# Batch 0 of a fused block-sparse attention and SwiGLU kernel: three groups of 256 queries in place of two of 384, with part of its data movement put on DMAs

## The chip, the cores and the metric

The kernel runs on one core of a Trainium2 chip. The metric is device microseconds (us) of one execution; the time before is the median of three runs. A core has five engines with a queue each: PE (TensorE, matrix products; its weight loads are listed as PEld), DVE (VectorE), ACT (ScalarE), POOL (GpSimd) and SP (SyncE). An instruction waits at the head of its queue until what it depends on is done, and all that stand behind it in that queue wait too. SP does nothing here but start DMAs, POOL does little else.

## What is computed

Attention over 4 batches of 8 heads, 768 positions and 64 features; then, over the 8 x 64 = 512 features of each position, an RMS norm and a gated feed-forward network (FFN):

```python
scores = scale * np.matmul(q, k.transpose(0, 1, 3, 2))        # q, k, v: (4, 8, 768, 64)
# mask, in blocks of 32: |blk_i - blk_j| <= 1, first and last block row and column, 3 sampled blocks a row
scores = np.where(mask, scores, -1000000000.0)
attn = softmax(scores);  x = np.matmul(attn, v)                # then (3072 tokens, 512)
xn = x / np.sqrt(np.mean(x * x, axis=-1, keepdims=True) + 1e-06) * rms_g
g = xn @ w_gate                                               # (512, 1536)
out = (g * sigmoid(g) * (xn @ w_val)) @ w_out                 # (1536, 512), float32
```

## The kernel before

**Groups.** `groups` is a list of eight (batch, half): each batch's 768 queries in two groups of `TG` = 384, that is three tiles of 128. The main loop (L501 on) goes through the groups, and in each through the 8 heads h.

**One head of one group.** `scores` (L276) makes the scores of two of the six key tiles: two matmuls from `KT` and `QT` into a PSUM tile `st` (two buffers), and one exponential on ACT into `ex`. It is called three times a head. `KT` and `QT` hold 64 rows of features and, under them, 24 rows (D:KR) that add the mask: block indicators for the keys (`kind`), 0 or -65536 for the queries (`qmask`). They exist twice, for batches of even and odd number. `pv` (L286) then makes 18 matmuls for the head *before* (its `ex` must be there), and DVE divides by the row sums into `stage`. After a group's last `pv`, `squares` sums the squares on DVE, `rms_power` (L307) raises them on POOL to `rstd`, `rms_scale` (L316) scales on DVE to `xs`, and `xs` is turned to `xg` with the features on the partitions: on PE (`transpose_x`, L328) for the first two groups and the last, else by DMA transposes that SP issues (L321), after a factor `gain` has been multiplied in.

**The FFN as filling.** A group's FFN (`ffn_pieces`, L344) is 36 pieces: for each of 12 slices of the hidden width a `gate` and a `val` of four matmuls each, then 12 pieces `down` of three matmuls. They go into a list `fill` when `xg` is ready, that is at head `TX` = 2 of the following group, and `position()`, called four times a head between `scores` and `pv`, takes 36/32 of a piece each time. So while PE works on group n's attention, it also works on group n-1's FFN. While there is no FFN (all of group 0, and group 1 up to head 2: `thin`), `keep_busy` (L142) puts matmuls of zeros in the gaps. `down`'s last part ends with a copy on ACT (`yo`) and the DMA to the output on SP (L387).

**Loads.** All loads of q, k, v and of the three weights go through POOL's queue, with a cast to bfloat16 except for v, in program order: batch 0's pairs of heads, `wg` and `wv` in two halves each, then at head 4 of group 0 two pairs of batch 1, then `wo` (L451). The first two heads come through SP (`first`). The mask rows of batch 0 are computed once and copied to the other heads by DVE (`copy_rows`, L216); those of the second `KT` and `QT` by two DMAs on SP (L454).

**Turning q and k.** q and k arrive with positions on partitions and are turned in pairs of heads. Batches 0 and 1: on PE (`transpose_qk`, L243: six transposes, then two copies on DVE), batch 1 at the places in `TURNS_0` (L488). Batches 2 and 3: `turn` (L261) starts a DMA transpose on SP into a buffer `turned`, and one head later `place` (L269) starts two DMAs on SP that copy from there to `KT` or `QT`. `place` must wait, at the head of SP's queue, until the transpose has landed. Four such turns stand in each group of 384:

```python
if turned:
    place(*next(iter(turned)))
if 0 < b < B - 1 and h >= 4:
    turn(b + 1, 2 * g + (h - 4) // 2, h % 2)
```

The order on every queue is that of the program: the schedule is written by hand (`tc.manual_schedule()`).

Of the kernel before, what the change touches and what calls it, by code (L numbers as in the profile page):

```python
# [17 lines left out]
def kernel(  # L18
# [30 lines left out]
    TG = HC * P  # L49
# [75 lines left out]
    def first_turn(t16, unread=None):  # L125
        t = ps_f.tile([P, HC, P], BF16, name="tfirst", tag="ff")
        for cc in range(HC):
            nc.tensor.transpose(
                out=t[:, cc, :], in_=t16[:, 2 * cc * D:(2 * cc + 2) * D], identity=ident)
        if unread is not None:  # L130
            keep_busy(2, 256, unread)
        return t

    def first_copy(h, which, t, w, copy):
        dst = (KT if which == 0 else QT)[0]
        view = dst[0:D, h, :].rearrange("p (c w s) -> p c w s", w=2, s=P)
        copy(out=view[:, :, w, :], in_=t[w * D:(w + 1) * D])
# [71 lines left out]
    def mask_queries(half):  # L209

        lo, hi = half * HC, (half + 1) * HC
        nc.vector.tensor_copy(
            out=qmask.rearrange("p (c r) -> p c r", c=NC)[:, lo:hi, :],
            in_=qnat[0:NB, :].rearrange("p (r c) -> p c r", c=NC)[:, lo:hi, :])
# [8 lines left out]
    mask_keys(0, 2)  # L223
# [8 lines left out]
    kt = first_turn(k16, unread)  # L232
    q16 = first_cast(0, 1)
    qt = first_turn(q16, unread)
    keep_busy(5, 256, unread)
    for which, t in ((0, kt), (1, qt)):
        first_copy(0, which, t, 0, nc.scalar.copy)
        first_copy(0, which, t, 1, nc.vector.tensor_copy if which else nc.scalar.copy)
    second16 = [first_cast(1, which) for which in range(2)]
    mask_keys(2, NC)  # L240


    def transpose_qk(b, pr, which, spare=False):  # L243


        src = (kbf if which == 0 else qbf).pop((b, pr))
# [3 lines left out]
        for e in range(2):  # L250
            for cc in range(HC):
                nc.tensor.transpose(  # L252
                    out=t[:, e, cc, :], in_=src[:, e, 2 * cc * D:(2 * cc + 2) * D],
                    identity=ident)
        view = dst[0:D, 2 * pr:2 * pr + 2, :].rearrange("p e (c w s) -> p e c w s", w=2, s=P)
        for w in range(2):
            nc.vector.tensor_copy(out=view[:, :, :, w, :], in_=t[w * D:(w + 1) * D])  # L257
# [18 lines left out]
    def scores(b, g, h, j2, ex):  # L276
        st = ps_s.tile([P, 2, 512], FP32, name="st", tag="st")
        for e in range(2):
            jt = 2 * j2 + e
            nc.tensor.matmul(  # L280
                out=st[:, e, 0:TG], lhsT=KT[b % 2][0:KR, h, jt * P:(jt + 1) * P],
                rhs=QT[b % 2][0:KR, h, g * TG:(g + 1) * TG], start=True, stop=True)
        nc.scalar.activation(  # L283
            out=ex[:, 2 * j2:2 * j2 + 2, :], in_=st[:, :, 0:TG], func=AF.Exp, scale=SCALE)

    def pv(b, h, ex, stage):  # L286
        op = ps_o.tile([P, HC, 80], FP32, name="op", tag="ot")
        for it in range(HC):
# [5 lines left out]
        nc.vector.reciprocal(out=rz, in_=op[:, :, D])  # L294
        nc.vector.tensor_tensor(  # L295
            out=stage[:, :, h * D:(h + 1) * D], in0=op[:, :, 0:D],
            in1=rz.unsqueeze(2).to_broadcast([P, HC, D]), op=ALU.mult)
# [9 lines left out]
    def rms_power(e):  # L307
        e["rstd"] = work.tile([P, HC], FP32, name="rstd", tag="rstd", bufs=2)
        nc.gpsimd.tensor_tensor(out=e["rstd"], in0=e["ssq"], in1=mhalf, op=ALU.pow)  # L309
        e["xs"] = work.tile([P, HC, DM], BF16, name="xs", tag="xs", bufs=2)  # L310
        e["xg"] = work.tile([P, KD, TG], BF16, name="xg", tag="xg", bufs=2)

    def by_dma(e):
        return e["bg"] not in (groups[0], groups[1], groups[-1])

    def rms_scale(e, it):  # L316
        if by_dma(e):
# [10 lines left out]
    def transpose_x(e, half):  # L328
        if by_dma(e):
            return  # L330
        xs, xg = e["xs"], e["xg"]
        t = ps_o.tile([P, 2, HC, P], BF16, name="tx", tag="ot")
        for w in range(2):
            c = 2 * half + w
            for it in range(HC):
                nc.tensor.transpose(  # L336
                    out=t[:, w, it, :], in_=xs[:, it, c * P:(c + 1) * P], identity=ident)
        for w in range(2):
            c = 2 * half + w
            nc.vector.tensor_scalar(  # L340
                out=xg[:, c, :], in0=t[:, w].rearrange("p c s -> p (c s)"),
                scalar1=rmsg[:, c:c + 1], scalar2=None, op0=ALU.mult)

    def ffn_pieces(gate_pool, b, g, xg, last=False):  # L344

        hps = work.tile([P, NF, TG], BF16, name="hps", tag="hps", bufs=2)
        held = {}

        def gate(f):
            gp = gate_pool.tile([P, 512], FP32, name="gp", tag="ff")  # L350
            for c in range(KD):
                nc.tensor.matmul(  # L352
                    out=gp[:, 0:TG], lhsT=wg[:, c, f * P:(f + 1) * P], rhs=xg[:, c, :],
                    start=(c == 0), stop=(c == KD - 1))
            th = work.tile([P, TG], BF16, name="th", tag="th", bufs=3)
            nc.scalar.activation(out=th, in_=gp[:, 0:TG], func=AF.Tanh, scale=0.5)  # L356
            held[f] = (gp, th)

        def val(f):
            gp, th = held.pop(f)  # L360
            vp = ps_f.tile([P, 512], FP32, name="vp", tag="ff")
            for c in range(KD):
                nc.tensor.matmul(  # L363
                    out=vp[:, 0:TG], lhsT=wv[:, c, f * P:(f + 1) * P], rhs=xg[:, c, :],
                    start=(c == 0), stop=(c == KD - 1))
            u = work.tile([P, TG], BF16, name="u", tag="u", bufs=3)
            nc.vector.scalar_tensor_tensor(  # L367
                out=u, in0=th, scalar=1.0, in1=gp[:, 0:TG], op0=ALU.add, op1=ALU.mult)
            nc.vector.tensor_tensor(out=hps[:, f, :], in0=u, in1=vp[:, 0:TG], op=ALU.mult)  # L369
# [5 lines left out]
        def down(tt, part, lo=0, hi=DM):  # L375
# [7 lines left out]
            if part == NQ - 1:  # L383
# [3 lines left out]
                nc.sync.dma_start(out=rows[g * HC + tt][:, lo:hi], in_=yo)  # L387
# [5 lines left out]
        for tt in range(HC):  # L393
            for part in range(NQ):
                if last and tt == HC - 1:
                    continue
                pieces.append(lambda tt=tt, part=part: down(tt, part))
        if last:
            for lo in range(0, DM, DM // 2):
                for part in range(NQ):  # L400
                    pieces.append(
                        lambda lo=lo, part=part: down(HC - 1, part, lo, lo + DM // 2))
# [3 lines left out]
    groups = [(b, g) for b in range(B) for g in range(2)]  # L406
    fill = []
    NPOS = 4 * H
    PER = 2 * NF + 4 * HC
    due = [0.0]  # L410

    def position():
        due[0] += PER / NPOS
# [8 lines left out]
    def after_pv(e, h):  # L422
        if h == H - 2:
            squares(e, 0, 0, (H - 1) * D)
        if h == H - 1:
            for it in range(HC):
                squares(e, it, (H - 1) * D, H * D)
            rms_power(e)


    def side_work(b, g, h):
        nb = b + 1
        if b == 0 and g == 0:
            if h % 2 == 0:
                cast_v(0, h // 2, nc.vector)
            if h == 0:
                copy_rows(KT, kind, 2, 4, 0, S)
                copy_rows(QT, qmask, 2, 4, 0, TG)
            if h == 1:
                load_gv(1)  # L440
            if h == 2:
                copy_rows(KT, kind, 4, H, 0, S)
            if h == 3:
                copy_rows(QT, qmask, 4, H, 0, TG)
                mask_queries(1)
            if h == 5:
                copy_rows(QT, qmask, 1, H, TG, S)
            if h == 4:
                load_qk(1, 0)
                load_qk(1, 1)  # L450
                nc.gpsimd.dma_start(out=wo, in_=moe_w_out.rearrange("(c p) f -> p c f", p=P))  # L451
            if h == H - 2:
                for T in (KT, QT):
                    nc.sync.dma_start(  # L454
                        out=T[1][D:KR, :, :],
                        in_=T[0][D:KR, H - 1, :].unsqueeze(1).to_broadcast([NB, H, S]))
            return
        if b == 0:
            if h == 1:
                load_v(1, 0)  # L460
                load_v(1, 1)
                for pr in range(2, NP):
                    load_qk(1, pr)
                nc.gpsimd.dma_start(
                    out=gain, in_=moe_rms_g.unsqueeze(0).to_broadcast([P, DM]))
            return

    def casts(b, g, h):


        if (b, g) == (0, 1):
            if h >= 6:
                cast_v(1, h - 6, nc.vector)
                load_v(1, h - 4)
            return
        if b == 0 or h not in (2, 4):
            return
        n = h // 2 - 1
        if g == 0:
# [3 lines left out]
        if b + 1 < B:  # L483
            load_v(b + 1, 2 * g + n)
            load_qk(b + 1, 2 * g + n)


    TURNS_0 = {(0, 1, 3): (0, 0), (0, 1, 4): (0, 1), (0, 1, 5): (1, 0), (0, 1, 6): (1, 1),  # L488
               (0, 1, 7): (2, 0), (1, 0, 0): (2, 1), (1, 0, 3): (3, 0), (1, 0, 4): (3, 1)}

    def turns(b, g, h):
        if (b, g, h) in TURNS_0:
            transpose_qk(1, *TURNS_0[(b, g, h)])
        if turned:
            place(*next(iter(turned)))
        if 0 < b < B - 1 and h >= 4:
# [4 lines left out]
    for gi, (b, g) in enumerate(groups):  # L501
# [3 lines left out]
            "bg": (b, g),  # L505
        }
        for h in range(H):
            ex = work.tile([P, NC, TG], BF16, name="ex", tag="ex", bufs=3)
            thin = gi == 0 or (gi == 1 and h <= TX)
            scores(b, g, h, 0, ex)  # L510
            if h == 0 and prev is not None:
                squares(prev[0], 2, 0, (H - 1) * D)
            if gi == 0 and h == 0:
                scores(b, g, h, 1, ex)
                second = [first_turn(t16) for t16 in second16]
                for which in range(2):
                    for w in range(2):
                        first_copy(1, which, second[which], w, nc.vector.tensor_copy)
                copy_rows(KT, kind, 1, 2, 0, S)
                copy_rows(QT, qmask, 1, 2, 0, TG)  # L520
                nc.vector.tensor_scalar(out=rmsg, in0=rmsg, scalar1=float(DM) ** 0.5,
                                        scalar2=None, op0=ALU.mult)
            if h == 1 and ending is not None:
                rms_scale(ending, 1)
            if h == TX and ending is not None:
                transpose_x(ending, 0)
            if gi == 0 and 0 < h < H - 2:
                transpose_qk(0, h // 2 + 1, h % 2, spare=True)
# [3 lines left out]
            if gi or h:  # L532
                scores(b, g, h, 1, ex)
            side_work(b, g, h)
            position()
            if h == 1 and ending is not None:
# [3 lines left out]
            if prev is not None:  # L540
                pe, pb, ph, pex = prev
                pv(pb, ph, pex, pe["stage"])
                after_pv(pe, ph)
                if ph == H - 1:
                    ending = pe
            position()
            scores(b, g, h, 2, ex)
            if gi == 0 and h == 0:
                transpose_qk(0, 1, 0, spare=True)
            position()  # L550
            if h == TX and ending is not None:
                transpose_x(ending, 1)
                fill.extend(ffn_pieces(ps_f, *ending["bg"], ending["xg"]))
                ending = None
            casts(b, g, h)
            turns(b, g, h)
            if gi == 2 and h == 0:
                nc.vector.tensor_scalar(out=gain, in0=gain, scalar1=float(DM) ** 0.5,
                                        scalar2=None, op0=ALU.mult)
            if h == 0 and ending is not None:  # L560
                rms_scale(ending, 0)
            if h == H - 1:
                squares(cur, 1, 0, (H - 1) * D)
            prev = (cur, b, h, ex)
    pe, pb, ph, pex = prev
    squares(pe, 2, 0, (H - 1) * D)
    pv(pb, ph, pex, pe["stage"])
# [15 lines left out]
    with tc.tile_pool(name="ps_tail", bufs=4, space=bass.MemoryType.PSUM) as ps_tail:  # L583
        for piece in ffn_pieces(ps_tail, *groups[-1], pe["xg"], last=True):
# [31 lines left out]
```

## Time and profile before

| what | value |
|---|---|
| median of three runs | 321.73 us (321.05 to 322.42) |
| the profiled execution's own time | 322.85 us |
| its span in the profile | 321.0 us |
| granted TensorE clock, mean | 0.995 |
| busy: PE, PEld, DVE, ACT, POOL | 309.9, 190.1, 208.9, 205.5, 47.1 us |
| first `gate` matmul of group 0 | 40.71 us after the span's start |
| first output DMA issued | 72.47 us |

The profile lists, per engine, what ran when, for how long, and what released each wait; times are from the span's start. "PEclk" is the clock that TensorE was granted, as a share of full speed. A PE instruction's listed duration is from its issue to the end of its results; in a stream the next one starts earlier, so that what one costs is read from the starts: four matmuls with 384 columns start 0.65 us apart from the next four. SPq rows are DMA starts in SP's queue, and their time is that of the issue, not that of the transfer. "q0" is the DMA queue fed by POOL, "q1" that fed by SP.

### The profile page before, as it was taken

Reading aid. Unit: us, or ns where it says so; the run is one execution under the profiler, and the core shown is the slowest. Engines: PE = TensorE matmul, PEld = TensorE weight load, DVE = VectorE, ACT = ScalarE, POOL = GpSimd, SP = SyncE. Lnnn points to the kernel's source line nnn. Section 1 sums busy time; section 2 is a strip of 40 time slices with the busy share of each in tenths; the row PEclk is TensorE's granted clock in tenths of the full one; section 3 lists DMA queues with packets and bytes.
Section 4 is the critical chain, followed back from the end, with each engine's and each line's share of the span. In section 5 each row is a group of like instructions: output and inputs, shape, how many; then the busy total and the mean of one; then the engine's idle time right before and its main releaser. Section 6 shows DMA issues by size and latency. Waiting matters only on the chain.

```text
span 321.0 us, 6990 instructions
## 1 busy us (share of the span) xinstructions
PE 309.9 (97%) x2779; PEld 190.1 (59%) x2779; DVE 208.9 (65%) x532; ACT 205.5 (64%) x321; POOL 47.1 (15%) x69
## 2 busy tenths in 40 slices
PE   8798799999999999999999999999999999999996
PEld 4465466655666556665566556665666556655554
DVE  6896667993787726684477727684477726693860
ACT  6678776655766667666766667666866667633322
POOL 9730600010220121100220121101000100010000
PEclk9889999999999999999999999999999999999999
DMA  7999994111696567837775456845200040002002
GB/s 153 297 219 224 210 257 82 45 55 67 131 140 84 65 173 131 166 63 108 163 124 100 92 149 117 151 88 107 66 2 0 19 133 0 2 1 100 1 0 100
DMA packets 52637, 33.57 MB, mean 105 GB/s; under 512 B 35620, under 2 KB 48316, under 8 KB 52604
## 3 DMA queue, kind: packets, MB, share of 16 engines
q0 software_dynamic: 13696, 17.17, 27.7%
q1 hardware_dynamic: 38872, 15.94, 22.5%
q8 instruction: 22, 0.36, 0.5%
q14 instruction: 11, 0.09, 0.1%
q10 hardware_dynamic: 36, 0.01, 0.0%
HBM read 28.59 MB, written 6.29 MB: 109 GB/s over the span
## 4 chain that ended last, share of the span: by engine, by line
PE 79%; DVE 12%; DMA 4%; POOL 1%; issue 1%; ACT 1%; SPq 0%; DVEq 0%; POOLq 0%
PE gp L352 18%; PE vp L363 17%; PE st L280 16%; PE yp L380 15%; PE op L290 10%; DVE junk L302 3%; DMA xg<-xs 2%; DMA vraw<-in_v_dram 2%; DVE hps L369 2%; DVE u L367 2%; DVE stage L295 1%; PE tqk L252 1%; PE unread L147 1%; PE tx L336 1%; DVE QT L257 1%
## 5 line engine op out<-in xcount | busy, mean ns | idle before, releaser
L283 ACT ACTIVATE ex<-st 128x768 bf16<-128x768 f32 x192 | 154.0, 811 | 57.2 <-PE st L280 54.5
L280 PE MATMUL st<-QT,KT 88*128 88x384 bf16 x384 | 93.8, 329 | 3.8 <-DVE QT L257 1.7
L352 PE MATMUL gp<-xg,wg 128*128 128x384 bf16 x384 | 78.4, 325 | 0.4 <-DMA xg<-xs 0.4
L363 PE MATMUL vp<-xg,wv 128*128 128x384 bf16 x384 | 78.1, 325 | 0.0
L367 DVE SCALAR_TENSOR_TENSOR u<-th,gp 128x384 bf16<-128x384 bf16 x96 | 53.0, 552 | 36.8 <-ACT th L356 35.5
L380 PE MATMUL yp<-wo,hps 128*128 128x512 bf16 (+1 forms) x300 | 73.8, 370 | 0.5 <-DVE hps L369 0.5
L356 ACT ACTIVATE th<-gp 128x384 bf16<-128x384 f32 x96 | 46.9, 489 | 35.4 <-PE gp L352 35.3
L369 DVE TENSOR_TENSOR hps<-u,vp 128x384 bf16<-128x384 bf16 x96 | 53.2, 554 | 10.4 <-PE gp L352 0.5
L280 PEld LDWEIGHTS <-KT 88*128 88x128 bf16 x384 | 36.6, 99 | 33.9 <-issue 4.4
L290 PEld LDWEIGHTS <-ex 128*128 128x128 bf16 x1152 | 45.4, 98 | 12.0 <-DVE KT L257 0.5
L363 PEld LDWEIGHTS <-wv 128*128 128x128 bf16 x384 | 36.2, 97 | 23.4
L352 PEld LDWEIGHTS <-wg 128*128 128x128 bf16 x384 | 35.7, 97 | 23.7 <-issue 0.9
L290 PE MATMUL op<-Vp,ex 128*128 128x65 bf16 x1152 | 47.7, 195 | 0.1
L380 PEld LDWEIGHTS <-hps 128*128 128x128 bf16 x300 | 27.7, 97 | 24.0 <-DVE hps L369 1.0
L294 DVE RECIPROCAL rz<-op 128x3 f32<-128x3 f32 x64 | 11.3, 177 | 32.3 <-PE op L290 32.1
L309 POOL TENSOR_TENSOR rstd<-ssq,mhalf 128x3 f32<-128x3 f32 x8 | 6.9, 867 | 145.8 <-DVE ssq L302 145.8
L386 ACT ACTIVATE yo<-yp 128x512 f32<-128x512 f32 (+1 forms) x25 | 14.4, 577 | 18.0 <-PE yp L380 18.0
L79 POOL DMA_DIRECT2D vraw<-in_v_dram x16 | 12.1, 755 | 89.5 <-DVE Vp L100 89.2
L295 DVE TENSOR_TENSOR stage<-op,rz 128x192 bf16<-128x192 f32 x64 | 22.9, 357 | 2.2
L302 DVE CUSTOM_DVE_ANT_0 junk<-stage 128x448 bf16<-128x448 bf16 x24 | 14.9, 623 | 0.6
L147 PE MATMUL unread<-idle 128*128 128x512 bf16 (+1 forms) x35 | 12.8, 406 | 1.2 <-DVE idle L140 1.2
L318 DVE SCALAR_TENSOR_TENSOR xs<-stage,rstd,gain 128x512 bf16<-128x512 bf16 x15 | 10.4, 747 | 5.3 <-POOL rstd L309 5.3
(60 smaller groups left out, 115.6 us busy)
## 6 DMA issues: line engine op xcount, KB each, us to landing
vraw<-in_v_dram POOLq DMA_DIRECT2D x16, 384.0 KB, 4.4
out_dram<-yo SPq DMA_DIRECT2D x23, 256.0 KB, 2.2
kbf<-in_k_dram POOLq DMA_DIRECT2D x15, 192.0 KB, 5.9
qbf<-in_q_dram POOLq DMA_DIRECT2D x15, 192.0 KB, 6.7
wg<-in_moe_w_gate_dram POOLq DMA_DIRECT2D x2, 768.0 KB, 13.7
wv<-in_moe_w_val_dram POOLq DMA_DIRECT2D x2, 768.0 KB, 18.1
wo<-in_moe_w_out_dram POOLq DMA_DIRECT2D x1, 1536.0 KB, 25.1
KT<-turned SPq DMA_DIRECT2D x16, 96.0 KB, 3.1
```

The costliest lines, as they stand in the source:

```text
L147: nc.tensor.matmul(out=t[:, 0:cols], lhsT=idle[:, 0:P], rhs=idle[:, 0:cols], start=True, stop=True)
L280: nc.tensor.matmul(out=st[:, e, 0:TG], lhsT=KT[b % 2][0:KR, h, jt * P:(jt + 1) * P], rhs=QT[b % 2][0:KR, h, g * TG:(g + 1) * TG], start=Tr ...
L283: nc.scalar.activation(out=ex[:, 2 * j2:2 * j2 + 2, :], in_=st[:, :, 0:TG], func=AF.Exp, scale=SCALE)
L290: nc.tensor.matmul(out=op[:, it, 0:VW], lhsT=ex[:, jt, it * P:(it + 1) * P], rhs=Vp[b % 2][:, h, jt, :], start=(jt == 0), stop=(jt == NC - 1))
L295: nc.vector.tensor_tensor(out=stage[:, :, h * D:(h + 1) * D], in0=op[:, :, 0:D], in1=rz.unsqueeze(2).to_broadcast([P, HC, D]), op=ALU.mult)
L302: nc.vector.tensor_tensor_reduce(out=junk[:, 0:hi - lo], in0=part, in1=part, scale=1.0, scalar=(e["ssq"][:, it:it + 1] if lo else DM * 1e- ...
L352: nc.tensor.matmul(out=gp[:, 0:TG], lhsT=wg[:, c, f * P:(f + 1) * P], rhs=xg[:, c, :], start=(c == 0), stop=(c == KD - 1))
L356: nc.scalar.activation(out=th, in_=gp[:, 0:TG], func=AF.Tanh, scale=0.5)
L363: nc.tensor.matmul(out=vp[:, 0:TG], lhsT=wv[:, c, f * P:(f + 1) * P], rhs=xg[:, c, :], start=(c == 0), stop=(c == KD - 1))
L367: nc.vector.scalar_tensor_tensor(out=u, in0=th, scalar=1.0, in1=gp[:, 0:TG], op0=ALU.add, op1=ALU.mult)
L369: nc.vector.tensor_tensor(out=hps[:, f, :], in0=u, in1=vp[:, 0:TG], op=ALU.mult)
L380: nc.tensor.matmul(out=yp, lhsT=hps[:, f, tt * P:(tt + 1) * P], rhs=wo[:, f, lo:hi], start=(f == 0), stop=(f == NF - 1))
```

## The change

Batch 0 becomes three groups of 256 queries (two tiles); batches 1 to 3 keep two of 384. So there are nine groups, and every function takes the group's tile count n. With it:

- `scores` of a 256-group takes three key tiles at once, so that a head has two exponentials of the same 768 columns in place of three. Its FFN has 32 pieces (8 of them `down`), and `enter` sets the rate anew for each group: 32 pieces over 36 positions for group 0, else over 32.
- Group 0's FFN enters one head earlier, at head 1 of group 1.
- Of batch 0's q, only the first 256 queries are turned ahead of their heads; the rest of the first two heads at heads 6 and 7 of group 0, that of the other pairs at heads 0, 2, 4 of group 1. The copies of one of them go to ACT.
- The mask rows of heads 2 to 7 of batch 0 come by two DMAs on SP, those of the other 512 queries and of the second `KT` and `QT` by three more at head 5.
- `wo` is loaded straight after `wg` and `wv`; batch 1's first q and k come after it, in group 1.
- Batch 1's q and k are turned by DMA: eight `turn`s at the eight heads of group 2 (`FIRST - 1`), each `place` one head later; batch 1's v is cast earlier.
- The first two groups have 256 queries now, so `xs` of the third third of batch 0 is turned by DMA.

```diff
+    groups = [(0, c, 2) for c in range(0, NC, 2)]
+    groups += [(b, c, HC) for b in range(1, B) for c in range(0, NC, HC)]
+    FIRST = NC // 2
...
     second16 = [first_cast(1, which) for which in range(2)]
-    mask_keys(2, NC)
+    mask_keys(HC, NC)
+    for T, m, hi in ((KT, kind, S), (QT, qmask, 2 * P)):
+        nc.sync.dma_start(out=T[0][D:KR, 2:H, 0:hi],
+                          in_=m[:, 0:hi].unsqueeze(1).to_broadcast([NB, H - 2, hi]))
...
+    def scores(grp, h, part, ex):
+        b, c0, n = grp
+        tg = n * P
+        nj = 2 if n == HC else 3
...
+    def enter(e, positions):
+        fill.extend(ffn_pieces(ps_f, e["grp"], e["xg"]))
+        rate[0] = len(fill) / positions
...
     def position():
-        due[0] += PER / NPOS
+        due[0] += rate[0]
...
+        if gi == 0:
             if h % 2 == 0:
                 cast_v(0, h // 2, nc.vector)
-            if h == 0:
-                copy_rows(KT, kind, 2, 4, 0, S)
-                copy_rows(QT, qmask, 2, 4, 0, TG)
             if h == 1:
                 load_gv(1)
-            if h == 2:
-                copy_rows(KT, kind, 4, H, 0, S)
...
+                nc.gpsimd.dma_start(out=wo, in_=moe_w_out.rearrange("(c p) f -> p c f", p=P))
+            if h in (3, 4):
+                mask_queries(h - 2)
             if h == 5:
-                copy_rows(QT, qmask, 1, H, TG, S)
...
+                nc.sync.dma_start(
+                    out=QT[0][D:KR, 1:H, 2 * P:S],
+                    in_=qmask[:, 2 * P:S].unsqueeze(1).to_broadcast([NB, H - 1, S - 2 * P]))
+                for T, m in ((KT, kind), (QT, qmask)):
+                    nc.sync.dma_start(out=T[1][D:KR, :, :],
+                                      in_=m.unsqueeze(1).to_broadcast([NB, H, S]))
+        if gi == 1:
+            if h == 1:
+                load_qk(1, 0)
                 load_v(1, 0)
                 load_v(1, 1)
+                load_qk(1, 1)
...
-    TURNS_0 = {(0, 1, 3): (0, 0), (0, 1, 4): (0, 1), (0, 1, 5): (1, 0), (0, 1, 6): (1, 1),
-               (0, 1, 7): (2, 0), (1, 0, 0): (2, 1), (1, 0, 3): (3, 0), (1, 0, 4): (3, 1)}
-
-    def turns(b, g, h):
-        if (b, g, h) in TURNS_0:
-            transpose_qk(1, *TURNS_0[(b, g, h)])
+    def turns(gi, b, g, h):
         if turned:
             place(*next(iter(turned)))
+        if gi == FIRST - 1:
+            turn(1, h // 2, h % 2)
         if 0 < b < B - 1 and h >= 4:
             turn(b + 1, 2 * g + (h - 4) // 2, h % 2)
...
+        tx = 1 if gi == 1 else TX
```

## The prediction

> **What bounds the kernel now.** I read the page first. PE is busy almost throughout:
>
> ```profile
> PE 309.9 (97%) x2779; PEld 190.1 (59%) x2779; DVE 208.9 (65%) x532; ACT 205.5 (64%) x321; POOL 47.1 (15%) x69
> ```
>
> But busy includes `keep_busy`. The stretches tell where PE is truly full, and the clock:
>
> ```profile
> 25.94:33.45 7.51, 6.45 (x80) 4.05 (x79) 4.47 (x16) 6.64 (x10) 0.00 (x0) 1.00 1.16 223
> 154.00:190.00 36.00, 36.00 (x326) 22.18 (x325) 22.57 (x57) 24.56 (x39) 4.83 (x7) 1.00 0.60 121
> 16.00:17.00 1.00, 1.00 (x5) 0.39 (x4) 0.99 (x3) 0.22 (x1) 0.41 (x2) 0.50 1.16 224
> ```
>
> (Stretch, length, busy of PE, PEld, DVE, ACT, POOL, clock, DMA share, GB/s.) From 25.94 three heads without FFN take 7.51 us, 2.50 each: ACT is nearly full, PE has zeros in its gaps. From 154, with FFN, PE is full. At 16 the clock is half. So time is won by starting the FFN earlier, or by taking work off PE after that; each PE stall after that costs its length. The timeline of PE gives the border:
>
> ```profile
> 40.71 0.99 PE L352 MATMUL gp<-xg,wg 128*128 128x384 bf16 x4
> ```
>
> **Prices**, from starts in PE's timeline. Four matmuls of 384 columns 0.65 us, so 0.108 for 256 columns; three `down` 0.65; 18 of `pv` 0.57 (27.34 to 27.91), so 12 in 0.38; six transposes 0.33 (45.37 to 45.70), 0.055 each; a `keep_busy` 0.22. So a head of 384 costs PE 0.98 + 0.57 = 1.55, one of 256 costs 1.03; a 256-wide `gate` or `val` 0.43.
>
> **Start of the FFN.** Head 2 is the first that needs the new mask DMAs. DVE can finish `kind` at 6.7 (the rows to 6.91 with less work in them). SP then needs 1 us to issue. How long such a DMA takes beside loads shows at the same kind of DMA before, issued at 18.30 (the timeline; then the DMA view of 18.3 to 22 and of 22 to 26):
>
> ```profile
> 18.30 1.01 SPq L454 DMA_DIRECT2D KT<-KT  x1
> ```
> ```profile
> q0 software_dynamic: 519, 0.77, 116.0%
> ```
> ```profile
> q0 software_dynamic: 435, 0.64, 88.7%
> q1 hardware_dynamic: 201, 0.29, 24.5%
> ```
>
> For 3.7 us nothing of q1 moves; then about 200 packets land in under 4 us. The new pair has 144 packets of 1536 bytes and 144 of 512: 6.7 + 3.7 = 10.4, then between 3 us (by bytes) and 5 (by packets): 13.5 to 15.4. I take 14.8, as loads fill q0 from 6 us on too (1.2 of full in 7 to 8). Without that wait head 2 would start at 12.0 (DVE's cast of v ends at 10.8, two copies of 0.55 follow). Before, it started at 14.28.
>
> The Trainium skill, "DMA: Bandwidth & Descriptors", section "Queues, rings and completion order", says that each engine takes turns between queues packet by packet. By that the rows would come at 12 at the latest; the 3.7 us here speak against it. It is rival C.
>
> The half clock at 15 to 18 follows a PE gap (12.56 to 14.28) in the trace; the new gap is longer, so I charge the same again, 1.2 us (head 2 took 3.6 before, a later one 2.5). Heads 2 to 7: ACT needs 2 x 0.74 + 0.29 gap = 1.76, PE 1.6 to 1.8: six at 1.77 = 10.6. Head 0 of group 1 to the end of `pv`: 1.7. From there to the first gate it was 7.8 (32.92 to 40.71); with two tiles for three in squares, xs and xg, and no `pv` between the halves of `transpose_x`, the same rows add up to 5.5. Sum 14.8 + 1.2 + 10.6 + 1.7 + 5.5 = 33.8: **6.9 us earlier**. Between 31.0 (mask rows at 12.0) and 34.4.
>
> **Work that moves behind that point.** Before it lay 11.3 heads' scores and 10 `pv` of 384 (16.8 us), after 10.5 and 9 of 256 (10.3): +6.5. Off PE go eight turns of batch 1, -2.6 (their 16 DVE copies, 8.9 us, bring nothing: DVE is 63% busy from 154). Second q parts of two pairs, +0.4; `transpose_x` of group 1, -0.2. Net **+4.1**. The other edits I cost at nothing: `wo` is issued about 7 us earlier and wanted near 52 (it landed at 46.3); the q rows for group 1 are issued near 21, land by 7.5 us later, wanted at 29; if that cover fails, each costs its lateness. wv's first half landed at 26.3, wanted at 34.
>
> **SP's queue, the new wait.** Batch 1 is turned in group 2 by eight turn-and-place steps, and all stand in SP's queue behind or between other DMAs: first turn, then group 0's first output, then the places and seven more turns, then the two DMA transposes of group 2's `xs` that the FFN needs at head 3 of group 3. The output waits for ACT's `yo`. The trace shows SP caught like that:
>
> ```profile
> SPq L387 <- ACT yo L386: 48.6, 2, 45.4
> ```
>
> So the chain cannot start before that `yo`, however early q and k lie there. What a step costs is in SP's timeline, in a stretch with few loads:
>
> ```profile
> 100.28 1.27 SPq L274 DMA_DIRECT2D QT<-turned  x2
> 101.65 1.29 SPq L265 DMA_TRANSPOSE turned<-kbf  x1
> 104.52 1.27 SPq L274 DMA_DIRECT2D KT<-turned  x2
> 105.88 1.29 SPq L265 DMA_TRANSPOSE turned<-qbf  x1
> 110.35 1.27 SPq L274 DMA_DIRECT2D QT<-turned  x2
> ```
>
> Place, turn, wait until the turn has landed, place: two steps in 10.07 us. The other three such stretches give 9.9, 9.8, 9.1: c = 4.86 a step. The fastest single step is 4.15 (2.8 + 1.36), the mean of all sixteen, loads beside them, 5.6.
>
> Supply, from the end of the matmuls of group 0's first output: yo and output 1.5, first place 1.4, seven steps 7c, two xs transposes 1.3 + 2.4 = 6.6 + 7c. PE's work to the place where `xg` is wanted: rest of head 1 none; head 2 of group 2 1.03 + 1.95 + 0.44 = 3.4; heads 3 to 7, 20 pieces, 5 x 1.03 + one `down` + 20 x 0.43 = 14.4; heads 0 to 2 of group 3, 3 x 1.55 + 4 x 0.43 + 8 x 0.65 = 11.6; 0.3 for the first scores: 29.7. PE is in order, so its `gate` at the head of the queue stops all scores and `pv` behind it, and ACT and DVE with them. Wait = 7c - 23.1: **10.9 us** at 4.86; 6.0 at 4.15, 16.1 at 5.6. It would be zero at c = 3.3, below any step here. After it the clock: the rows at 15 to 18 us lost (14.0 to 18.0: 0.31 + 0.5 + 0.5 + 0.4) **1.7**.
>
> The Trainium skill, "TensorE: Matmul & The Clock Gate", section "What's actually happening", has the clock halved after an idle window of some 3.4 us until a busy one of that length; the trace agrees as to half and to about 3.5 us. By its figures the loss would be 1.7 too, and without a throttle my sum 1.7 less.
>
> **Sum** against the profiled execution, 322.85 (span 321.0 and 1.85 around it): -6.9 + 4.1 + 10.9 + 1.7 = +9.8, 332.7. The median shown is 1.1 lower; on that footing 321.73 + 9.8 = **331.5 us**. Its own range, by c: 326.6 to 336.7.
>
> **Rivals.**
> A. *The chain of turns is hidden*, the mechanism that ends on the other side: if steps overlap to c below 3.3, or the chain starts at k's landing (46 to 55 us) and not behind the output, the xs transposes come in time. Then -6.9 + 4.1: 318.9. For it: SP was in time in all groups before (the wait for `xg` was 0.4). Against: there it had four steps in 36 us, here seven in 30.
> B. *256-wide pieces starve PE.* `val` of the next slice needs the PSUM buffer that `u` frees. From the end of a gate to that `val` PE has 1.6 us of work (two pieces, scores or `pv`); gate to end of u takes 1.15 with ACT free, 1.95 behind an exponential. 0.3 in each of 22 pairs is 6.6; half of it falls ahead of the `xg` wait and is swallowed: +3.3, 334.8. For: th and u have such waits now (35 us each in all). Against: PE does not wait for them at 384.
> C. *Mask rows come by turns with the loads*: head 2 at 12.0 and no throttle there, 4.0 less: 327.5, with the `xg` wait as forecast.
> D. *Only a short wait for xg is left* (2 to 4 us): within 0.5%, 321 to 323.
> That the change does not do what it says: the program's order shows the groups, the five mask DMAs and the eight turns as described; not a case.
>
> **Chances.** Forecast 0.60, A 0.15, B 0.09, C 0.09, D 0.07. Faster by over 0.5% (what a measurement of this kernel can tell from none) is A, 0.15; same is D, 0.07; slower the rest, 0.78. The range 320.0 to 338.0 takes in the forecast's bounds, B, C and most of D, and leaves A and what is above out, some 0.2.
>
> **What would show it.** Right: PE without work for 6 to 16 us at the first gate of the third group (near 87 us), released by `xg<-xs`; SP busy with turn and place from the first output (near 57) until then; clock 0.5 after it; the first gate of all near 34; head 2's scores waiting for the mask DMAs until about 14.8, clock down again. Wrong: no idle PE near 87 (A); gaps after `gate` or before `val` all through groups 1 and 2 (B); head 2 at 12 (C). The forecast falls if SP's steps are shorter than every one of before, or if the first output comes much sooner than 23 us after the first gate.

## The result

| what | before | after |
|---|---|---|
| median | 321.39 us (320.89 to 322.42, 4 runs) | 338.27 us (337.47 to 339.05, 4 runs) |
| the profiled execution's own time, its span | 322.85, 321.0 us | 338.15, 336.4 us |
| mean clock | 0.995 | 0.970 |
| first `gate` of all | 40.71 us | 36.57 us |
| first output DMA issued | 72.47 us | 59.58 us |

The change makes the kernel 5.2% slower: after/before is 1.0521 [1.0483, 1.0558]. Forecast were 331.5 us and 320.0 to 338.0, so the time lies 6.8 us above the forecast and 0.3 us above the range. Ratios, here and below, leave out executions that fell into a slower state of the chip; medians and ranges keep them.

The first part and the second of the page of after, PE's rows and its clock alone. Each digit is a slice of 8.4 us:

```profile
PE 308.3 (92%) x2865; PEld 202.1 (60%) x2865; DVE 203.9 (61%) x561; ACT 206.6 (61%) x334; POOL 47.1 (14%) x70
...
PE   8398899999508999999999999999999999999996
...
PEclk9879999999956999999999999999999999999999
```

PE is busy for as long as before (308.3 us for 309.9), in a span that is 15.4 us longer. Two holes account for it: slice 2, and slices 11 and 12, each with a lower clock in it or just after it. The waits of PE in after (in all, times, longest) name them:

```profile
PE gp L379 <- DMA xg<-xs: 13.4, 1, 13.4
PE st L299 <- DMA QT<-QT: 5.1, 1, 5.1
```

Where they lie, in PE's timeline (start, length; in brackets the idle time before and its releaser):

```profile
17.08 0.80 PE L299 MATMUL st<-QT,KT 88*128 88x256 bf16 x3 [5.14 <-DMA QT<-QT]
...
36.57 0.60 PE L379 MATMUL gp<-xg,wg 128*128 128x256 bf16 x4
...
102.36 0.40 PE L379 MATMUL gp<-xg,wg 128*128 128x256 bf16 x1 [13.36 <-DMA xg<-xs]
```

At 17.08 head 2 of group 0 gets its mask rows; at 102.36 the first gate of the third group gets `xg`. After each the stretches show the half clock (a stretch, its length, the busy time of PE, PEld, DVE, ACT and POOL, then clock, DMA share and GB/s: the clock is the third number from the right):

```profile
17.00:21.00 4.00, 3.92 (x30) 2.93 (x31) 1.84 (x5) 1.62 (x2) 1.23 (x2) 0.53 1.13 235
...
105.00:106.00 1.00, 1.00 (x18) 0.94 (x16) 0.43 (x2) 0.00 (x0) 0.00 (x0) 0.50 0.04 4
```

And SP's queue, which the second wait comes from: first output, first place, then turn and place by turns, the last place, and only then the transposes of `xs`:

```profile
59.58 0.37 SPq L414 DMA_DIRECT2D out_dram<-yo  x1
60.05 1.38 SPq L284 DMA_DIRECT2D KT<-turned  x2
61.52 1.29 SPq L275 DMA_TRANSPOSE turned<-qbf  x1
64.38 1.27 SPq L284 DMA_DIRECT2D QT<-turned  x2
...
89.58 1.27 SPq L284 DMA_DIRECT2D KT<-turned  x2
90.94 1.78 SPq L275 DMA_TRANSPOSE turned<-qbf  x1
97.16 1.27 SPq L284 DMA_DIRECT2D QT<-turned  x2
98.53 1.26 SPq L346 DMA_TRANSPOSE xg<-xs  x1
```

From place to place it takes 4.33, 6.37, 5.32, 5.07, 4.22, 4.22, 7.58, mean 5.30 us (60.05 to 97.16 in seven).

### The profile page after: what moved, and what is told of

Its sections match the earlier page's. It is cut to its first block, busy times and chain, and to the rows that moved or that the text cites. A ratio compares the mean times of both kernels' runs of the same rounds, so it can differ in the third digit from the quotient of the medians.

```text
span 336.4 us, 7271 instructions
## 1 busy us (share of the span) xinstructions
PE 308.3 (92%) x2865; PEld 202.1 (60%) x2865; DVE 203.9 (61%) x561; ACT 206.6 (61%) x334; POOL 47.1 (14%) x70
## 3 DMA queue, kind: packets, MB, share of 16 engines
q1 hardware_dynamic: 53252, 19.81, 28.3%
## 4 chain that ended last, share of the span: by engine, by line
PE 76%; DMA 11%; DVE 6%; SPq 4%; issue 1%; ACT 0%; POOL 0%; DVEq 0%
PE gp L379 17%; PE vp L390 17%; PE st L299 16%; PE yp L407 16%; PE op L311 10%; DMA turned<-qbf 5%; DMA turned<-kbf 3%; SPq L284 3%; DMA QT<-QT 3%; DVE junk L323 2%; DMA xg<-xs 1%; DVE stage L316 1%; PE unread L151 1%; DVE KT L208 0%; PE tqk L262 0%
## 5 line engine op out<-in xcount | busy, mean ns | idle before, releaser
L299 PE MATMUL st<-QT,KT 88*128 88x384 bf16 (+1 forms) x432 | 95.4, 312 | 5.5 <-DMA QT<-QT 5.1
L379 PE MATMUL gp<-xg,wg 128*128 128x384 bf16 (+1 forms) x432 | 80.8, 309 | 13.5 <-DMA xg<-xs 13.4
L394 DVE SCALAR_TENSOR_TENSOR u<-th,gp 128x384 bf16<-128x384 bf16 (+1 forms) x108 | 54.8, 508 | 55.9 <-ACT th L383 54.3
L390 PE MATMUL vp<-xg,wv 128*128 128x384 bf16 (+1 forms) x432 | 80.6, 309 | 0.4 <-DVE u L394 0.4
L383 ACT ACTIVATE th<-gp 128x384 bf16<-128x384 f32 (+1 forms) x108 | 48.9, 453 | 41.9 <-PE gp L379 41.7
L396 DVE TENSOR_TENSOR hps<-u,vp 128x384 bf16<-128x384 bf16 (+1 forms) x108 | 55.0, 509 | 12.3 <-PE vp L390 0.9
L299 PEld LDWEIGHTS <-KT 88*128 88x128 bf16 x432 | 41.9, 99 | 31.1 <-issue 5.7
L315 DVE RECIPROCAL rz<-op 128x3 f32<-128x3 f32 (+1 forms) x72 | 12.5, 173 | 30.9 <-PE op L311 30.7
L331 POOL TENSOR_TENSOR rstd<-ssq,mhalf 128x3 f32<-128x3 f32 (+1 forms) x9 | 7.3, 816 | 155.6 <-DVE ssq L323 155.6
L316 DVE TENSOR_TENSOR stage<-op,rz 128x192 bf16<-128x192 f32 (+1 forms) x72 | 24.1, 335 | 2.5
```

Source lines behind the costliest of these rows:

```text
L299: nc.tensor.matmul(out=at[:, e, 0:tg], lhsT=KT[b % 2][0:KR, h, jt * P:(jt + 1) * P], rhs=QT[b % 2][0:KR, h, c0 * P:c0 * P + tg], start=Tru ...
L316: nc.vector.tensor_tensor(out=stage[:, 0:n, h * D:(h + 1) * D], in0=op[:, 0:n, 0:D], in1=rz[:, 0:n].unsqueeze(2).to_broadcast([P, n, D]), ...
L379: nc.tensor.matmul(out=gp[:, 0:tg], lhsT=wg[:, c, f * P:(f + 1) * P], rhs=xg[:, c, 0:tg], start=(c == 0), stop=(c == KD - 1))
L383: nc.scalar.activation(out=th[:, 0:tg], in_=gp[:, 0:tg], func=AF.Tanh, scale=0.5)
L390: nc.tensor.matmul(out=vp[:, 0:tg], lhsT=wv[:, c, f * P:(f + 1) * P], rhs=xg[:, c, 0:tg], start=(c == 0), stop=(c == KD - 1))
L394: nc.vector.scalar_tensor_tensor(out=u[:, 0:tg], in0=th[:, 0:tg], scalar=1.0, in1=gp[:, 0:tg], op0=ALU.add, op1=ALU.mult)
```

## The experiments

The first theory, S: the eight turn-and-place steps in SP's queue make group 2's `xs` transposes late, and without them the 13.4 us and the half clock behind them come back. Its rival, K: the steps only stand in for a lateness that another wait will show. For the 5.1 us there were M1, the mask DMAs stand behind what POOL had queued, and M2, such a DMA is slow by itself. Ratios are to the kernel before, on the same chip.

**1. Take `xs` of the third group out of SP's queue** (turn it on PE):

```diff
-not in (groups[0], groups[1], groups[-1])
+not in (groups[0], groups[1], groups[2], groups[-1])
```

> The third group of batch 0 has its xs turned on PE (eight transposes, 0.44 us) in place of the two DMA transposes that stand behind the eight turns in SP's queue; all else as in the changed kernel (338.3 us). Theory S (SP's queue of turns delays xg): the wait of 13.4 us at the first gate of that group and the half clock after it (2 us) go, 0.4 us of PE come: 323.4. The last places then decide: q of heads 6 and 7 was placed at 97.2 and would be wanted at 98.4, so up to 2.5 us may stay as a wait of head 6's scores: 323 to 326. Rival B (256-wide pieces or the work moved behind the FFN's start cost the time): little changes, over 333. Rival K (the wait moves from xg to the rows of K and Q of batch 1): a wait of 5 us or more at heads 4 or 6, 328 to 332.

Measured: 335.07 us (333.25 to 340.2), 1.0394 [1.0324, 1.0463]. By the ratios (1.0521 in after) that is some 4 us for a 13.4 us wait. PE's timeline and SP's show where it went:

```profile
104.21 0.80 PE L299 MATMUL st<-QT,KT 88*128 88x384 bf16 x2 [5.57 <-DMA QT<-turned]
```
```profile
98.72 1.27 SPq L284 DMA_DIRECT2D QT<-turned  x2
...
101.27 1.74 SPq L275 DMA_TRANSPOSE turned<-kbf  x1
...
118.80 2.39 SPq L284 DMA_DIRECT2D QT<-turned  x2
121.71 1.22 SPq L346 DMA_TRANSPOSE xg<-xs  x1
```

The last place (98.72) now holds up the scores that need it, head 6 of group 3. Batch 2's four turns come behind it, and so group 3's `xs` as well: a third wait of 4.0 us. The 323 to 326 of S failed. K is right about where the wait goes, though 335.07 is above its 328 to 332: SP's queue as a whole is behind, whichever of its clients waits.

**2. Issue group 0's outputs elsewhere**, so that the chain need not wait for `yo`: from ACT's queue as shown, or from POOL's (`nc.gpsimd` for `nc.scalar`).

```diff
-nc.sync.dma_start(out=rows[c0 + tt][:, lo:hi], in_=yo)
+(nc.scalar if grp == groups[0] else nc.sync).dma_start(
+    out=rows[c0 + tt][:, lo:hi], in_=yo)
```

> Group 0's two output DMAs are issued from ACT's queue in place of SP's; all else as in the changed kernel. Theory S says that the chain of turns was held until 59.6 us only by the first output that stood ahead of it in SP's queue: now it goes on as soon as the first turn has landed, near 51, eight us earlier, with slower steps while batch 1's loads still land (5.3 to 5.6 each). The wait for xg falls from 13.4 to 3 to 7 us: 328 to 332. If the chain was not held by the output but by loads or by DMA time, the wait stays above 11 and the time above 336.

> Group 0's two outputs go through POOL's queue; all else as in the changed kernel. On ACT's queue they stopped ACT for 10.9 us, which made that run no test of the claim that the first output holds SP's chain. There the first turn, issued at 47.0, had landed only at 56.2, so the output can have held the chain from about 56.2 to 59.6 at most: 3.4 us. Expected now: chain from 56.2, wait for xg 10, 334.9 (334 to 336). If the output holds nothing, 338; if it holds as much as the prediction said (from the landing of k near 48), the wait is under 4 and the time 328 or less.

Measured: ACT 347.1 us (344.1 to 347.45), 1.0766 [1.0706, 1.0825], far above the 328 to 332 expected; POOL 336.29 (333.75 to 342.09), 1.0423 [1.0367, 1.0479], near the 334 to 336 expected, but not for the reason given: the wait for `xg` was 4.1 us and not 10. With ACT the output stood at the head of ACT's queue until 70.35, though its `yo` was done before 60, and the exponentials behind it stood too (the waits of ACT):

```profile
ACT ex L302 <- DMA KT<-turned: 10.9, 1, 10.9
```

Why an output issued there waits for a transfer of SP's I haven't settled. With POOL, SP's timeline is:

```profile
47.44 1.33 SPq L275 DMA_TRANSPOSE turned<-kbf  x1
56.65 1.73 SPq L284 DMA_DIRECT2D KT<-turned  x2
...
92.32 1.27 SPq L284 DMA_DIRECT2D QT<-turned  x2
```

Even with nothing between, the first place comes 9.2 us after its turn. So of the time before the chain in after, only 60.05 - 56.65 = 3.4 us is the output's; in after itself the turn issued at 48.19 landed 9.4 us later, near 57.6, which leaves the output 2.4. The rest is the landing of the first turn, beside the loads. The `xg` wait fell by 9.3 us: 3.4 by the start, 1.4 by steps of 5.10 for 5.30, and the rest by another PE wait of 4.2 ahead of it, at 64.38, which takes back as much. That wait comes from POOL's queue:

```profile
POOL qbf L75 <- DMA turned<-qbf: 12.5, 1, 12.5
```

A load of q stood at the head of POOL's queue until 61.81, when a turn on SP had landed, and `rstd` stood behind it; in after the same load was issued at 50.62. The kernel with the outputs on ACT has the same wait. So moving the outputs moved a second thing too, and neither run shows the price of the output alone. What they do show is that the chain is too long from either start.

**3. The mask rows**: made by DVE instead of the two early DMAs; or the two DMAs kept, and POOL's loads after the first three held until DVE has computed `kind` (a copy on POOL that reads it; the loop stood at the top before).

```diff
-    for T, m, hi in ((KT, kind, S), (QT, qmask, 2 * P)):
-        nc.sync.dma_start(out=T[0][D:KR, 2:H, 0:hi],
-                          in_=m[:, 0:hi].unsqueeze(1).to_broadcast([NB, H - 2, hi]))
...
+            if h == 0:
+                copy_rows(KT, kind, 2, 4, 0, S)
+                copy_rows(QT, qmask, 2, 4, 0, 2 * P)
+            if h == 2:
+                copy_rows(KT, kind, 4, H, 0, S)
+            if h == 3:
+                copy_rows(QT, qmask, 4, H, 0, 2 * P)
```
```diff
+    held_back = const.tile([P, 1], BF16, name="held_back")
+    nc.gpsimd.tensor_copy(out=held_back[D:KR, :], in_=kind[:, S - 1:S])
+    for pr in range(1, NP):
+        if pr + 1 < NP:
+            load_qk(0, pr + 1)
+        load_v(0, pr)
+    load_gv(0)
```

> The mask rows of heads 2 to 7 of batch 0 (keys, and queries of group 0) are copied by DVE as in the kernel before, in pieces ahead of heads 2 and 4, and the two early DMAs on SP are gone; the later three stay. Theory M (head 2 waits for these DMAs until 17.1, 5.1 us, and then runs at half clock): head 2 starts near 12.7, no throttle, first gate at 31 to 32 in place of 36.6, the wait for xg as it was (13 us, all its terms move together): 332.5 to 334. Rival D (DVE then is late with copies of K and mask rows): head 2 near 14.5, half clock stays, first gate at 34 to 35: 336.

> The mask DMAs stay on SP, but POOL holds back all loads after the first pair of k and q and the first v until the mask rows are computed (a copy of one column on POOL reads them), so that the loads' queue holds less when the mask DMAs are issued at 7.1. Theory M1 (a DMA of SP's queue waits for what POOL's loads have queued before it): the rows move within 1.5 us of the issue and head 2 starts at 12 to 13; the later loads come 2 us later, which the weights can bear; first gate near 32, 333 to 335. Theory M2 (these copies are slow in themselves, 288 packets from 24 partitions): nothing moves before 11 and head 2 starts at 15.5 or later; 337 or more.

Measured: DVE 334.48 us (333.38 to 336.1), 1.0398 [1.0345, 1.0452], first gate at 32.74. Held loads 333.67 (332.62 to 334.2), 1.0361 [1.031, 1.0412], first gate at 31.34. Both take back some 4 to 5 us and leave the `xg` wait at 13.2; with DVE time and first gate come half a us or more above what was expected (332.5 to 334, 31 to 32), with held loads both are as expected. In after SP had issued the mask DMAs at 7.11 and 8.17; in the held kernel at the same 7.11 and 8.17, but there head 2 started at 13.17 and waited for DVE:

```profile
13.17 0.49 PE L303 MATMUL st<-QT,KT 88*128 88x256 bf16 x3 [0.67 <-DVE KT L271]
```

The DMA view of after for 10 to 11 and for 12 to 13 us, then that of the held kernel for 9 to 10 (packets, MB, share):

```profile
q0 software_dynamic: 227, 0.20, 123.9%
...
q0 software_dynamic: 158, 0.14, 78.9%
q1 hardware_dynamic: 80, 0.12, 38.0%
```
```profile
q1 hardware_dynamic: 74, 0.11, 60.8%
q0 software_dynamic: 50, 0.09, 35.1%
```

In after no q1 packet moves from 9 to 11 us; the rows start near 12, 5 us after the issue, and land at 17. M1 is right: ahead of 7.11 POOL had issued seven loads in after and three in the held kernel, whose fourth came at 7.68. Behind the three, the same two DMAs were moving by 9 to 10 us. How the delay grows with the loads isn't settled: in the kernel before, eight loads were under way at 18.30 and the first packet came after 3.7 us, not 5.

**4. Take batch 1's turns out of SP's queue**: all eight on PE in group 2 as before, or only those of pairs 2 and 3 (as shown; all eight have `h >= 0`).

```diff
-            turn(1, h // 2, h % 2)
+            if h >= 4:
+                transpose_qk(h // 2, h % 2, 0, HC, False, nc.vector.tensor_copy, b=1)
+            else:
+                turn(1, h // 2, h % 2)
```

> All eight turns of batch 1 go back to PE (six transposes and two DVE copies each), at the heads of group 2 where the changed kernel issues its DMA turns; the rest is the changed kernel. The run before this showed that the wait only moves to the next thing behind SP's chain (to q of heads 6 and 7, 5.6 us, and to xg of the group after, 4.3), so theory S is now: SP's queue as a whole is behind, by 8 steps of about 5.3 us that the four turns of batch 2 follow. Without the eight: no wait for xg or for K and Q in groups 2 to 4, no half clock there, PE +2.6: 338.3 - 13.4 - 2.0 + 2.6 = 325.5, up to 327 for waits on the one PSUM buffer. Rival W (what costs is the split in three with its moved work): 331 or more.

> Half of them: the four turns of heads 4 to 7 (pairs 2 and 3) go to PE, those of pairs 0 and 1 stay on SP. Theory S, steps of 5.3 us: SP is through its four near 77, ahead of the xs of group 2 (wanted at 88.8), so the wait is gone in full: 338.3 - 15.4 + 1.3 = 324.2. If the wait were proportional to the turns left on SP (half), 331.

Measured: eight 340.85 us (339.85 to 342.45), 1.0596 [1.055, 1.0641]; four 338.0 (336.45 to 338.7), 1.051 [1.0469, 1.0551]. Both expectations failed, and with them S: group 2's `xg` came in time in both, but nothing was won. A wait of 7.4 (8.7) us stands one group later, at the first gate of group 3, and PE has the turns to do. The waits of PE for `xg`, first with eight turns on PE, then with four:

```profile
PE gp L378 <- DMA xg<-xs: 7.7, 2, 7.4
PE gp L378 <- DMA xg<-xs: 9.0, 2, 8.7
```

That batch 2's chain in SP's queue is too long by itself was hidden in after by the longer wait ahead of it.

**5. Both ends at once.** Four turns on PE and held loads; all eight on PE and mask rows by DVE.

> The same with POOL's loads held back until the mask rows are computed, as in the run where head 2 came at 13.2 in place of 17.1 (4.5 us less). The two causes are far apart in time, so they add up: 324.2 - 4.5 = 319.7, a little under the kernel before (321.1). If the wait for xg only hid other waits of an earlier start (loads of wo and batch 1), 322 to 324.

> The three groups nearly alone: batch 1 turned on PE as in the kernel before (eight turns, in group 2), the early mask rows copied by DVE, no early mask DMAs. If only SP's eight extra turns and the mask DMAs cost time, this is the kernel before less 7 us of earlier FFN start plus 6.7 us of PE work behind it: 321. Theory S2 (a group whose neighbour has a 256-wide FFN passes in about 28 us on PE, while SP's four turns of the next batch, the landing of their loads ahead and the xs transposes behind need 35): the wait of 7 to 9 us at the first gate of group 3 of the runs with turns on PE stays, with 2 us of half clock and some 3 us of small waits at the one PSUM buffer: 331 to 336.

Measured: 332.53 us (331.72 to 336.67), 1.0358 [1.0286, 1.043], against 319.7 or 322 to 324 expected; and 337.26 (336.21 to 338.95), 1.0487 [1.0446, 1.0528], which is above 331 to 336, so even the second theory was too low there. PE and SP in the first of the two:

```profile
122.71 0.80 PE L382 MATMUL gp<-xg,wg 128*128 128x384 bf16 x2 [7.45 <-DMA xg<-xs]
```
```profile
83.97 3.85 SPq L417 DMA_DIRECT2D out_dram<-yo  x2
92.32 1.22 SPq L278 DMA_TRANSPOSE turned<-kbf  x1
95.14 1.31 SPq L287 DMA_DIRECT2D KT<-turned  x2
...
112.80 1.27 SPq L287 DMA_DIRECT2D QT<-turned  x2
114.17 2.58 SPq L349 DMA_TRANSPOSE xg<-xs  x2
```

This gives the second theory, S2. SP's work for batch 2 runs from 83.97 to the landing of `xg` at 122.7: wait for the outputs and for batch 2's first k to land (92.32), four turn-and-place steps to 114.1, `xs` behind them. PE reaches the place where `xg` is wanted at 122.71 - 7.45 = 115.26. The kernel before has the same work of SP in the first half of batch 1, and there it was in time; its first turn, its `xs` transposes and the gate that needs them:

```profile
87.22 1.32 SPq L265 DMA_TRANSPOSE turned<-kbf  x1
...
111.72 2.57 SPq L321 DMA_TRANSPOSE xg<-xs  x2
```
```profile
117.45 0.82 PE L352 MATMUL gp<-xg,wg 128*128 128x384 bf16 x4
```

Count both from the first gate of the group before (80.50 there, 86.94 here). SP's first turn comes 6.7 us after it there and 5.4 here, `xs` 31.2 and 27.2: SP is no slower here. PE wants `xg` 37.0 us after that gate there, and 28.3 here, where `xg` lands only after 35.8. In the later groups, too, PE needs 36 us from first gate to first gate; in group 3 the filling is the FFN of 256 queries, and PE passes in 29 (first gates at 88.80 and 117.65 in the first kernel of experiment 6). The group whose FFN was made narrow is the one that SP has no time for.

**6. The test of S2**: four turns on PE and held loads, as in 5, and group 3's `xs` on PE too (`groups[3]` in the list of experiment 1), so that nothing PE wants in that group stands behind SP's chain. Beside it the same with all eight turns on PE.

> As the run with four turns on PE and loads held (332.5), and the xs of group 3, too, turned on PE (twelve transposes, 0.66 us), so that it no longer stands behind batch 2's four turns in SP's queue. Theory S2: the wait of 7.45 at group 3's first gate and the 1.9 of half clock go, nothing else waits: 323.3, 322 to 324.5. If SP is behind from there on (as when the third group's xs alone went to PE), the wait moves on to group 4's xg or to K and Q of batch 2: 328 or more.

> The same with all eight turns of batch 1 on PE (1.3 us more of PE than with four, and more waits at the one PSUM buffer that they share with pv): 325 to 326 by theory S2. SP has nothing to do in group 2 but two outputs then, so if the time were set by SP before batch 2, this would be the faster one.

Measured: 323.68 us (322.13 to 324.75, 9 runs), 1.006 [1.0038, 1.0082], inside 322 to 324.5; and 327.07 (325.91 to 329.06), 1.017 [1.0138, 1.0202], 1 us above what was expected; there head 2 waited 1.6 us for its mask rows again. In the first, PE's timeline has no bracket at the two gates that waited:

```profile
88.80 0.60 PE L382 MATMUL gp<-xg,wg 128*128 128x256 bf16 x4
...
117.65 0.99 PE L382 MATMUL gp<-xg,wg 128*128 128x384 bf16 x4
```

One line (`xs` of group 3) takes 332.53 to 323.68: 8.9 us (9.6 by the ratios) for a wait of 7.45 and the half clock behind it, less the PE time of the transposes. S2 is borne out. What is left is no gain. In the profiled run the first gate is at 32.94, 7.8 earlier than before; the moved work is +4.1, four turns on PE 24 x 0.055 = +1.3, `xs` on PE 12 x 0.055 = +0.7. Sum -1.7; measured is 322.0 - 321.0 = +1.0. Of the 2.7 between, 1.3 is idle time of PE: after the first gate it is idle for 5.97 us there and for 4.63 in before. The rest I could not place. No kernel run here beats the kernel before.

## Why the prediction was right in kind and wrong in size

Sign, place and mechanism held: slower, by a wait for the third group's `xg` at the end of a chain of turns in SP's queue, with the half clock behind it, and the first output starting the chain (59.58 is 23.0 after the first gate; forecast some 23). That it was the output was close to luck: the prediction took the first turn to be ready early, and it landed near 57.6, 2.4 us before the chain began. The ledger, in the profiled executions' spans:

| term | forecast | measured | from |
|---|---|---|---|
| FFN starts earlier | -6.9 | -4.1 | 40.71 to 36.57 |
| work moved behind it | +4.1 | +4.2 | not measured: what the other rows leave of 15.4 |
| wait for `xg` | +10.9 | +13.4 | the wait |
| half clock after it | +1.7 | +1.9 | 0.5 from 102.36 to 106.0, 0.94 for 1 us more |
| sum | +9.8 | +15.4 | 321.0 to 336.4 |

A count supports the second row: after its first gate, after has 288 score matmuls of 384 columns and 80 of 256 for 317 of 384, 1044 of `pv` for 972, and 28 transposes for 72, which at the prediction's prices is +3.8.

Two terms of the sum were mis-sized, the start of the FFN and the step c; the path and the mechanism were right.

- **Start of the FFN**, mis-sized by 2.8. The step "6.7 + 3.7 = 10.4, then between 3 us (by bytes) and 5 (by packets): 13.5 to 15.4. I take 14.8": issued at 7.11, the rows moved near 12, after 4.9 us and not 3.7, then took 5 to land, and head 2 started at 17.08, 2.3 us late. The row of before that I took, 3.7 us without a packet, had as many loads under way (eight, for seven here); why the delay was longer here stays open. The page of the Trainium skill on "DMA: Bandwidth & Descriptors", section "Queues, rings and completion order", would have had the queues take turns and the rows in time. From 9 to 11 us this case's trace doesn't agree (q1 none, q0 over 100%), unless the rows' packets were not yet there to take their turn, which the trace doesn't show. From 12 us on it does (q1 38.0%, q0 78.9%), and with the loads held already at 9 (q1 60.8%, q0 35.1%). So rival C was wrong and the forecast still too mild.
- **c**, mis-sized by 0.44 a step. "What a step costs is in SP's timeline, in a stretch with few loads": the chain here does not lie in such a stretch. The four stretches priced leave out the first step from place to place of each group, 9.64 us (90.64 to 100.28), 7.28, 8.48 and 7.63. The seventh step, beside the loads of batch 2, took 7.58, and the second, with an output between, 6.37; without these two the mean is 4.63. The mean of all steps of before "loads beside them, 5.6" was the nearer row. By the formula, 7 x 5.30 - 23.1 = 14.0; measured 13.4.
- **A** fell: PE idled for 13.4 us. **B** fell: the waits of `val` for u were 0.4 us in the whole of after, and the pieces of 256 columns do not starve PE. **D** fell: the wait was not 2 to 4 us.
- **The range** stopped at 338.0. By its own bounds c at 5.6 and the first gate at 34.4 give 336.7 + 0.6 = 337.3, so it left 0.7 us for all else, and the first gate came 2.2 us behind that bound.
- **The medians** are 16.9 us apart and the spans 15.4. The profiled execution of before has the half clock of 15 to 18 us (mean 0.995, span 321.0); in 10 of 14 executions of the kernel before, made beside the second kernel of experiment 5 and those of experiment 6, the clock is 0.998 or more and the span 319.1 to 319.9, once 320.4. So the 1.1 us between that execution and the median were probably this throttle; the clocks of the executions behind that median are not known. After does not escape it: its four executions have 0.968 to 0.970, and its profiled one lies 0.1 us below the median. So the step "on that footing", which took 1.1 us off the sum, was wrong by as much.
- **Not foreseen**: that SP has too little time for batch 2's four steps as well. In a prediction of the single change this did not show, since the first wait covers it; it decides what undoing the first wait is worth. "SP was in time in all groups before" was read for the 36 us groups and not carried to the 29 us ones beyond group 2.

## What to carry to other kernels

When a group of work is made smaller, list every queue's work for that group and compare each with the new, shorter time: what was hidden in 36 us need not be in 29. A step priced in a quiet stretch has to be priced again where it will run. Where one in-order queue is behind as a whole, moving one client out of it only shows the next; count the queue's total, and expect the first repair to return little.

## What the runs showed of the hardware

- Two DMAs issued on SP's queue at 7.11 and 8.17 began to move near 12 and landed at 17 behind seven loads that POOL had issued, and landed by 13 behind three.
- A DMA transpose took 9.2 us from its issue to that of the place behind it beside loads (47.44 to 56.65, POOL's variant of experiment 2), and 2.82 with few of them (92.32 to 95.14, the first kernel of experiment 5).
- An output issued on ACT stopped its exponentials for 10.9 us: the busy engine paid for the issue's wait, whose cause is open, more than for the issue (0.38 us).
- In the first kernel of experiment 5 a wait of 7.45 us gave back 8.9 when it was removed, though PE took on 0.7 of work for it; the half clock after the wait (0.5 from 122.71 to 128) is part of its price.
